# Two more groups of products summed to one chunk on VectorE, a new written order, and x tiles split over two queues

## The chip, the cores and the metric

The kernel runs on one core of a Trainium2 chip. The core has TensorE (PE: matmuls, and their weight loads, PEld), VectorE (DVE), ScalarE (ACT), GpSimd (POOL) and SyncE (SP, which issues most of the DMAs). Each works through its own queue of instructions in order and waits on semaphores where it needs another's result. The metric is the device time of one execution in microseconds, as a median over runs. A profiled execution has a span, from its first to its last instruction, which is a little shorter than its device time.

## The reference

With x of 2048 tokens x 512 columns in bf16, the result is x plus two branches of the same layer-normalised x:

```python
xn = _layernorm(x, axis=-1)
return x + _A_ref(xn, A_wqkv, A_wo) + _B_ref(xn, B_w_in, B_w_sp, B_b_sp, B_w_out)
```

Branch A is local dilated attention. q, k and v come from xn @ wqkv, in 32 heads of 16 columns. Each token attends to 8 tokens: itself and the seven at distances 2, 4, ... 14 before it. The logit is the dot product of q with each of the eight k over the 16 columns of a head; a softmax over the eight weighs the eight v; the result goes through wo.

Branch B is a gated MLP with a mixer over tokens. z = gelu(xn @ w_in) has 1376 columns. Its second half z2 is layer-normalised and multiplied from the left by the 2048 x 2048 matrix w_sp, with a bias per token (g = w_sp @ z2 + b_sp). The first half z1 is multiplied by g, and the product goes through w_out.

## The kernel before

Tokens stand in 16 tiles of 128. A tile's number is 4*tb + j: four token blocks tb of 512, each with four tiles j. The work is done by j ("block j" is the four tiles with the same j), in the order ORD = [1, 2, 3, 0] for the attention.

**The start** (L558 to L628) is written out by hand. Loads of x and of the q and k weights are issued first (L164 to L180): tile 0 as two halves of 64 partitions, on SP and ACT; tile 1 (tb=1, j=0) on ACT; tiles 2 and 3 of block 0 in one load on POOL; then on SP the q weights, block 1 of x, the k weights, blocks 2 and 3 of x, and w_z2. For each tile VectorE computes mean and variance (`ln_stats`, L201), ScalarE the square root (`ln_sqrt`), VectorE the reciprocal and the normalised tile (`ln_tile`). TensorE transposes it (`tr`), and ScalarE copies the transpose into xnT (`tr_copy`, L224); for later blocks a transposing DMA on SP does this (`tr_dma`). `qk_part` (L300) multiplies the q weights (m = 0, 1) or k weights (m = 2, 3) with some of the token blocks, in two halves cc of four chunks kc each, and `qk_copy` takes the result out of PSUM. Block 0 has the tiles 0 to 3 of the load above in its token blocks. `warm_up` matmuls keep TensorE running before the data is there.

**The rest** follows the string ORDER (L42), a list of steps, which L682 to L686 walk through. Every step issues its instructions on its engine, so ORDER is each engine's queue. A name has a letter for the step and numbers for its piece:

- On TensorE: `z` (matmuls of z2 for one tile), `X` (of z1), `q` (q or k of a block), `V` (v, eight pieces), `L` (logits), `G` (w_sp times z2 for one output tile; `G0.b` is a quarter of it), `O`, `Or`, `Oh` (the output: attention part, the rest and the main part of w_out).
- On ScalarE: `zg`, `Xg` (gelu out of PSUM), `zs` (squares for the variance), `qc`, `Vc`, `Lc` (copies out of PSUM), `Gi` (adds the bias), `E` (exp).
- On VectorE: `p` (products of q with four shifted k, for one group g and chunk c), `a`, `b` (pair adds, below), `nw`, `st` (small steps from sums to 1/std of z2), `N` (normalises a tile of z2), `M`, `S`, `R` (softmax), `U` (z1 times g), `A` (attention weights times v, 15 operations for each block), `F` (adds x to the output).
- On SP: `w` (transposing load of a tile of w_sp), `wo`, `late`, `xr` (loads), `T` (transposing DMA of a U), `s` (store).

**The logits.** There are eight groups g: four blocks, two halves of the eight shifts. A product tile pr has four chunks c of 128 columns. The sum over a head's 16 columns is made by TensorE (`logits`, L354): it multiplies each chunk by a 0/1 matrix, accumulating over the chunks that are left. `pair_add` (`a`) adds chunks 2, 3 onto 0, 1 on VectorE, leaving two; `pair_add2` (`b`) adds chunk 1 onto 0, leaving one. CHUNKS says how many chunks `L` still has to multiply, four matmuls for each:

```python
CHUNKS = (1, 1, 2, 2, 1, 1, 2, 2)
...
        n_c = CHUNKS[g]
        for c in range(n_c):
            for tb in range(TB):
                PE.matmul(pl[32 * tb:32 * tb + 32, :, :], rsel[:], pr[g % 3][:, c, :, tb, :],
```

So `b0`, `b1`, `b4`, `b5` stand in ORDER, and groups 2, 3, 6 and 7 have two chunks. Groups share three buffers (g % 3).

**What ties the queues together.** Matmul results go to a pool of three PSUM tiles (`z`, `X`, `q`, `V`, `G`, `O`) and one of two (`L`); a tile is free again when ScalarE or VectorE has read it. `G0.b` needs the `N` of block j = b; the other `G` need all of them. `N` needs `nw.13`, which needs all `zg` and `zs` of blocks 0 to 2. `U` n needs `Gi` n and `Xg` n; `T` n needs `U` n; `Or` and `Oh` of output block o need `T` 4o to 4o+3. `O` o needs `A` 15o+14. The w_sp tiles are loaded where q, k or logits data stood, after their last reader. exp and gelu use different tables of ScalarE, and changing from one to the other is a table load.

Of the kernel before, what the change touches and what calls it, by code (L numbers as in the profile page):

```python
# [70 lines left out]
def kernel(  # L71
# [145 lines left out]
    def tr(i):  # L217
        j, tb = i % 4, i // 4
        pt = ps_aux.tile([P, C, P], BF16, name="pt", tag="aux")
        for c in range(C):  # L220
            PE.transpose(pt[:, c, :], xall[:, j, tb, c * P:(c + 1) * P], ident[:])
        return pt

    def tr_copy(i, pt):  # L224
        A.copy(xnT[:, :, i * P:(i + 1) * P], pt[:])  # L225

# [72 lines left out]

    def qk_part(pq, j, m, b0, b1, ccs=(0, 1), p0=None):  # L300
        sd, c0 = m // 2, 2 * (m % 2)
        p0 = b0 if p0 is None else p0
        xv = xnT[:].rearrange("p k (b j t) -> p k b j t", b=TB, j=4)
        for cc in ccs:
            for kc in range(C):
                PE.matmul(pq[:, cc, p0 * P:(p0 + b1 - b0) * P], wqk[:, sd, kc, c0 + cc:D:C],  # L306
                          xv[:, kc, b0:b1, j, :], start=(kc == 0), stop=(kc == C - 1))
# [385 lines left out]
```

## Time and profile before

| | us |
|---|---|
| Time, median of 4 runs (204.63 to 206.45) | 204.82 |
| The profiled execution's own time | 204.79 |
| Its span | 203.1 |
| VectorE idle in the span | 18.1 |
| ScalarE busy | 102.6 |
| Table load, each of 12 | 1.28 |
| DMA, mean over the span | 128 GB/s |
| TensorE clock granted | 1.0 throughout |

In a row of the timeline, the columns are the start and the length in microseconds, the engine, the line of the kernel, the operation, out<-in with the shape, the number of instructions merged, and in brackets the idle time before it with what ended it. TensorE's matmuls are pipelined, so that the length of one is longer than its step; the distance from one start to the next is what a matmul costs in a row of them. Line numbers of the changed kernel are up to 8 higher.

### The profile page before, as it was taken

The numbers are of one execution on the slowest core, as the hardware profiler recorded it, in microseconds if no ns is written. First come the engines' busy times: TensorE is split into PE (matmuls) and PEld (weight loads), VectorE is DVE, ScalarE is ACT, GpSimd is POOL, SyncE is SP. The second block draws the span as 40 slices with busy tenths as digits, with TensorE's granted clock in tenths as the row PEclk, the third lists the DMA queues.
The fourth block names the chain that finished last, engine by engine and source line by source line (L and its number), as shares of the span: only waits on it lengthen the run. The fifth ranks groups of instructions, "written<-read, shape, count | busy, mean of one in ns | idle before, by whom it ended". The sixth has DMA issues, their size and how long they took to land.

```text
span 203.1 us, 4065 instructions
## 1 busy us (share of the span) xinstructions
PE 197.6 (97%) x1683; PEld 125.0 (62%) x1683; DVE 185.0 (91%) x263; ACT 102.6 (51%) x163; POOL 18.2 (9%) x15
## 2 busy tenths in 40 slices
PE   7899999999999999999999999999999999999993
PEld 2589856555666666666566666666654544664561
DVE  4989799999999999999899999999999999998504
ACT  3665978978999986923732273596230010021000
POOL 5000000799300000000000000000000000000000
PEclk9999999999999999999999999999999999999999
DMA  4972457900000397248990974969900384474463
GB/s 140 360 261 60 97 103 248 206 0 3 0 0 3 67 205 156 66 95 220 218 135 14 179 167 110 233 143 186 223 1 3 97 172 87 134 212 92 118 184 103
DMA packets 65826, 25.91 MB, mean 128 GB/s; under 512 B 56208, under 2 KB 65488, under 8 KB 65552
## 3 DMA queue, kind: packets, MB, share of 16 engines
q1 hardware_dynamic: 65360, 25.12, 55.3%
q0 software_dynamic: 80, 0.26, 0.5%
q8 instruction: 13, 0.21, 0.5%
q10 hardware_dynamic: 368, 0.27, 0.4%
q14 instruction: 5, 0.04, 0.1%
HBM read 10.13 MB, written 2.10 MB: 60 GB/s over the span
## 4 chain that ended last, share of the span: by engine, by line
PE 83%; DMA 6%; SPq 4%; DVE 3%; issue 2%; ACT 0%; DVEq 0%
PE pg L449 35%; PE pz L235 18%; PE pq L306 12%; PE pv L410 7%; PE po L521 4%; DMA r_w<-in_A_wqkv_dram 4%; PE po L497 4%; SPq L474 2%; PE pl L360 1%; DMA r_uz<-r_uz 1%; DVE r_pr L428 1%; DVE r_qk L511 1%; DMA out_dram<-r_qk 1%; SPq L469 1%; SPq L516 1%
## 5 line engine op out<-in xcount | busy, mean ns | idle before, releaser
L449 PE MATMUL pg<-z,r_qk 128*128 128x344 bf16 x448 | 67.0, 309 | 0.0
L449 PEld LDWEIGHTS <-r_qk 128*128 128x128 bf16 x448 | 43.8, 98 | 21.8
L235 PE MATMUL pz<-w_z,xnT 128*128 128x344 bf16 x256 | 40.0, 309 | 0.0
L424 DVE TENSOR_TENSOR r_pr<-r_x,r_w 128x2048 bf16<-128x2048 bf16 x32 | 38.3, 1221 | 1.2 <-PE pl L360 0.8
L455 ACT ACTIVATE gs<-pg,b_col 128x688 bf16<-128x688 f32 x16 | 13.3, 831 | 41.3 <-PE pg L449 31.7
L428 DVE TENSOR_TENSOR r_pr<-r_pr 128x2048 bf16<-128x2048 bf16 x28 | 33.9, 1218 | 0.0
L235 PEld LDWEIGHTS <-xnT 128*128 128x128 bf16 x256 | 24.9, 98 | 13.3 <-issue 0.8
L306 PE MATMUL pq<-xnT,r_w 128*128 128x256 bf16 (+1 forms) x176 | 28.7, 316 | 0.5 <-ACT xnT L225 0.3
L340 DVE TENSOR_TENSOR r_pr<-r_qk 128x2048 bf16<-128x2048 bf16 x24 | 28.0, 1221 | 0.0
L306 PEld LDWEIGHTS <-r_w 128*128 128x128 bf16 x184 | 20.2, 114 | 7.9 <-DMA r_w<-in_A_wqkv_dram 0.9
L297 ACT ACTIVATE r_uz<-pz 128x688 bf16<-128x688 f32 x16 | 11.7, 742 | 20.8 <-PE pz L235 20.6
L634 POOL CAST b_col<-b 128x16 f32<-128x16 bf16 x1 | 15.3, 15342 | 32.8 <-DMA b<-in_B_b_sp_dram 32.8
L316 ACT CAST r_qk<-pq 128x1024 bf16<-128x1024 f32 (+1 forms) x16 | 15.4, 990 | 4.7 <-PE pq L306 4.4
L521 PE MATMUL po<-r_w,r_uz 128*128 128x512 bf16 x70 | 15.8, 380 | 0.0
L511 DVE TENSOR_TENSOR r_qk<-po,r_qk 128x512 bf16<-128x512 f32 x14 | 9.1, 685 | 6.7 <-PE po L521 6.7
L497 PE MATMUL po<-r_lg,r_pr 32*128 32x512 bf16 x224 | 14.5, 375 | 0.0
L410 PE MATMUL pv<-xnT,r_w 128*32 128x512 bf16 x256 | 14.4, 380 | 0.0
L521 PEld LDWEIGHTS <-r_uz 128*128 128x128 bf16 x85 | 8.0, 98 | 9.8 <-issue 1.5
L349 DVE TENSOR_TENSOR r_pr<-r_pr 128x4096 bf16<-128x4096 bf16 x6 | 13.6, 2286 | 0.0
L259 ACT ACTIVATE junk<-z 128x688 bf16<-128x688 bf16 x16 | 12.5, 780 | 0.1
L253 ACT ACTIVATE z<-pz 128x688 bf16<-128x688 f32 x16 | 11.7, 739 | 1.5 <-PE pz L235 1.5
L203 DVE BATCH_NORM_STATS2 stats<-r_x 128x6 f32<-128x512 bf16 x16 | 10.7, 671 | 1.7 <-DMA r_x<-in_A_x_dram 1.7
(82 smaller groups left out, 177.0 us busy)
## 6 DMA issues: line engine op xcount, KB each, us to landing
r_qk<-in_A_x_dram SPq DMA_DIRECT2D x16, 128.0 KB, 2.4
r_lg<-in_A_wo_dram SPq DMA_DIRECT2D x8, 256.0 KB, 4.3
out_dram<-r_qk SPq DMA_DIRECT2D x15, 128.0 KB, 1.8
r_w<-in_A_wqkv_dram SPq DMA_DIRECT2D x3, 512.0 KB, 4.9
r_x<-in_A_x_dram SPq DMA_DIRECT2D x3, 512.0 KB, 6.2
w_z<-in_B_w_in_dram SPq DMA_DIRECT2D x2, 688.0 KB, 5.4
r_w<-in_B_w_out_dram SPq DMA_DIRECT2D x1, 640.0 KB, 5.4
r_x<-in_A_x_dram POOLq DMA_DIRECT2D x1, 256.0 KB, 3.9
```

The lines of the kernel that those rows point to most:

```text
L235: PE.matmul(pz[:, hh, 0:FHALF], xnT[:, kc, i * P:(i + 1) * P], wz[:, kc, hh * FHALF:(hh + 1) * FHALF], start=(kc == 0), stop=(kc == C - 1))
L306: PE.matmul(pq[:, cc, p0 * P:(p0 + b1 - b0) * P], wqk[:, sd, kc, c0 + cc:D:C], xv[:, kc, b0:b1, j, :], start=(kc == 0), stop=(kc == C - 1))
L316: cast = A.copy(dst, pq[:, :, p0 * P:(p0 + b1 - b0) * P].rearrange("p c (b t) -> p c b t", b=b1 - b0))
L340: prod = V.tensor_tensor(pr[g % 3][:, c].rearrange("p w b t -> p b w t"), q3.unsqueeze(2).broadcast_to([P, TB, 4, P]), k4, ALU.mult)
L349: V.tensor_tensor(pr[g % 3][:, 0:2], pr[g % 3][:, 0:2], pr[g % 3][:, 2:4], ALU.add)
L410: PE.matmul(pv[32 * tb:32 * tb + 32, dd, :], wv[:, kc, 2 * d2 + dd, :], xnT[:, kc, tb * TBS:(tb + 1) * TBS], start=(kc == 0), stop=(kc == ...
L424: V.tensor_tensor(pw_t[n], vp[:, :, off:off + P], a_sb[:, slot_w(w), ts].unsqueeze(1).broadcast_to([P, DH, P]), ALU.mult)
L428: V.tensor_tensor(pw_t[n] if dst is None else dst, pw_t[n], pw_t[m], ALU.add)
L449: PE.matmul(pg[:, hh, 0:FHALF], wsp[n][:, k, :], z2[:, k, hh * FHALF:(hh + 1) * FHALF], start=(k == 0), stop=(k == NT - 1))
L497: PE.matmul(pc, op[32 * tb:32 * tb + 32, d, o * P:(o + 1) * P], wo_r[32 * tb:32 * tb + 32, d, cs], start=(d == 8), stop=False, tile_positi ...
L521: PE.matmul(pc, uT[:, o % 2, m, tb * P:(tb + 1) * P], wout[:, m, cs], start=False, stop=(m == MCH - 3))
L634: G.tensor_copy(b_col[:], b16[:])
```

## The change

Three things change. CHUNKS has one chunk for groups 2 and 3 too, so the steps `b2` and `b3` come in and `L2` and `L3` have four matmuls instead of eight. ORDER is written anew. And the start is changed: tiles 0 and 1 of block 0 are loaded as halves of 256 columns, one half on SP and one on ACT; tiles 2 and 3 on ACT instead of POOL; the statistics of tiles 0 and 1 are made by halves; the transposes of tiles 0 and 1 are issued before their copies, and the copy of tile 1 is in two; the first q matmuls take chunks 0 and 1 before 2 and 3; and the matmuls for token block 2 of the first two q pieces, which were together with block 3, are put ahead of the k weights' first use.

```diff
-CHUNKS = (1, 1, 2, 2, 1, 1, 2, 2)
+CHUNKS = (1, 1, 1, 1, 1, 1, 2, 2)
 ORDER = """
-z1.3 z0.0 p1.1 z1.1 zg1.3 p0.0 zg0.0 q2.0 zg1.1 p0.1 q2.2 qc2.0 p1.0 p1.3 q2.3 qc2.2 p0.3 z3.1 p0.2 qc2.3
-zs1.1 z0.3 p1.2 zg3.1 z1.2 a0 w0 zg0.3 zs1.3 z1.0 zs0.3 a1 q3.1 zg1.2 w3 zg1.0 halo q2.1 zs0.0 b0 qc3.1 p2.0
-z2.2 qc2.1 b1 z2.0 p2.2 V0 zg2.0 p2.3 zg2.2 zs2.0 L1 L0 z0.1 Vc0 p3.3 Lc0 q3.3 p3.0 zs1.2 zg0.1 p2.1 q3.0
-qc3.3 p3.1 z0.2 a2 qc3.0 zs2.2 z2.3 zg0.2 q3.2 p3.2 zs1.0 zg2.3 a3 z3.0 qc3.2 z3.2 zg3.0 p4.3 zs2.3 z2.1 zg3.2
-p4.1 z3.3 zs0.2 p4.0 zg2.1 X3 zg3.3 nw.0 p4.2 X5 Xg3 nw.1 a4 Lc1 X4 Xg5 zs0.1 L2 zs2.1 V4 p5.3 zs3.1 st.0 Xg4
-nw.2 V3 nw.3 p5.2 Vc4 nw.4 p5.0 zs3.2 L3 V2 zs3.0 nw.5 nw.6 nw.7 Vc3 nw.8 nw.9 nw.10 p5.1 Lc2 V5 Lc3 nw.11 b4
-w4 Vc2 V1 nw.12 Vc5 a5 w2 zs3.3 V7 Vc1 nw.13 st.1 b5 w1 V6 Vc7 N0.0 N1.2 st.2 N1.0 N0.2 L4 L5 N0.3 X7 N1.1
-st.3 N2.0 st.4 Vc6 N0.1 X6 N1.3 N3.1 late N2.3 N3.2 G0.0 N3.0 Xg7 M0.0 G0.1 Xg6 N2.1 M0.1 N2.2 X1 M0.2 N3.3
-p7.1 G0.2 Xg1 M0.3 Lc4 G0.3 p7.3 G1 p6.0 E0 p7.2 Gi0 p6.3 Lc5 p6.2 G4 Gi1 w7 S0.0 p7.0 w6 p6.1 S0.1 xr0 S0.2
-G3 a7 S0.3 S0.4 Gi4 w5 a6 w10 R0 X0 Gi3 U4 L7 T4 L6 G2 A0 Xg0 Lc6 w8 U1 Lc7 U3 U0 A1 A2 X2 Gi2 mask M1.0 G5
...
-A22 Gi9 wo0.3 wo0.2 A23 Xg14 A24 U7 A25 S1.4 T7 X8 Gi14 A26 wo1.2 X9 wo0.0 wo0.1 A27 w12 G10 A28 Xg9 R1 Xg8
-A29 w13 A30 X13 A31 G11 Xg13 A32 Gi10 A33 U8 A34 A35 X11 Gi11 A36 O0 Xg11 A37 A38 U14 A39 Or0 Oh0.0 A40 A41
-Oh0.1 F0.0 U10 s0.0 F0.1 G13 F0.2 T8 A42 s0.1 F0.3 A43 s0.3 xr1 U11 A44 O1 w15 U9 A45 Gi13 A46 A47 Or1 Oh1.0
-A48 Oh1.1 F1.0 F1.1 A49 s1.1 s0.2 G12 T11 A50 A51 F1.2 F1.3 s1.2 s1.0 A52 xr2 X15 A53 G15 Xg15 A54 T10 Gi12
-A55 s1.3 T9 A56 U12 O2 Gi15 U15 U13 T15 A57 T13 A58 Or2 Oh2.0 T12 A59 Oh2.1 F2.0 F2.1 s2.1 T14 O3 F2.2 F2.3
-xr3 s2.0 Or3 s2.3 Oh3.0 s2.2 Oh3.1 F3.0 F3.1 s3.1 s3.0 end
+z1.2 z0.0 p1.3 z2.2 zg1.2 p1.0 zs1.2 q2.0 zg0.0 p0.2 zg2.2 z0.3 p0.3 zs2.2 q2.2 p1.2 qc2.0 zg0.3 p0.0 z0.2
+qc2.2 p1.1 zs0.0 z1.1 p0.1 zg0.2 z0.1 zg1.1 a1 q2.3 zg0.1 zs0.1 p2.0 q2.1 zs1.1 qc2.3 a0 halo z3.3 qc2.1 z1.3
+zg3.3 p2.2 zs0.2 z2.3 b1 zg1.3 z2.1 zg2.3 b0 z2.0 zg2.1 p2.3 zs0.3 z1.0 p2.1 zg2.0 L0 zs2.3 L1 z3.1 p3.2 zg1.0
+zs1.3 q3.2 nw.0 p3.0 zg3.1 nw.1 a2 Lc1 q3.0 qc3.2 zs2.1 z3.2 p3.3 qc3.0 zs2.0 q3.3 p3.1 zg3.2 p4.0 w1 zs1.0
+q3.1 qc3.3 nw.2 p4.1 w0 X0 nw.3 qc3.1 a3 z3.0 Xg0 w3 Lc0 X3 nw.4 b2 zg3.0 X1 nw.5 b3 w2 V6 nw.6 Xg1 nw.7 p4.3
+Xg3 zs3.3 nw.8 p4.2 L2 V2 Lc2 nw.9 Vc6 nw.10 a4 L3 zs3.0 V1 zs3.2 nw.11 st.0 Lc3 p5.2 V7 Vc2 nw.12 b4 zs3.1 V5
+Vc1 st.1 nw.13 M0.0 st.2 Vc7 p5.1 L4 V3 N2.0 M0.1 p7.3 st.3 Vc5 V0 N1.0 Vc3 M0.2 N1.2 N1.1 st.4 V4 N2.3 Vc0
+N0.3 N3.2 N1.3 N0.2 X2 N0.1 Vc4 N3.1 N0.0 X4 N3.0 N2.1 p7.2 G0.0 N2.2 p6.2 G0.1 Xg4 Xg2 N3.3 G0.2 p5.0 X5 p5.3
+G0.3 p6.0 w4 G1 M0.3 Gi0 Xg5 late p6.3 a5 E0 p6.1 G3 Gi1 w7 Lc4 U0 S0.0 w6 a6 X7 Gi3 b5 G2 p7.0 S0.1 p7.1 S0.2
+a7 S0.3 S0.4 L6 L5 G4 Lc6 U1 T0 R0 wo1.0 U3 Xg7 w9 A0 Gi2 Lc5 A1 T1 A2 L7 G7 Lc7 T3 Gi4 mask A3 w10 A4 M1.0
+wo1.2 A5 X9 Gi7 U4 A6 T4 X11 U2 G6 w8 Xg11 A7 Xg9 A8 w5 A9 A10 xr0 G9 M1.1 Gi6 A11 M1.2 A12 M1.3 A13 X6 w15
+A14 G8 Xg6 A15 Gi9 A16 A17 E1 X8 S1.0 wo0.2 Gi8 wo0.3 wo1.1 X12 A18 wo0.0 T2 G10 A19 A20 Xg12 Xg8 U9 A21 wo0.1
+S1.1 wo1.3 U7 X10 A22 Gi10 G15 U6 A23 T6 S1.2 w13 A24 A25 S1.3 w14 S1.4 G5 R1 A26 Xg10 T7 Gi15 A27 A28 A29 O0
+Gi5 w11 A30 A31 U5 Or0 A32 Oh0.0 A33 U8 Oh0.1 F0.0 F0.1 U10 G13 F0.2 F0.3 A34 xr1 A35 s0.2 A36 T5 X15 A37 Gi13
+s0.0 w12 G11 A38 Xg15 A39 T8 A40 s0.1 A41 s0.3 T9 A42 O1 Gi11 A43 U11 A44 Or1 A45 Oh1.0 A46 Oh1.1 F1.0 F1.1
+U15 G12 F1.2 T15 A47 A48 F1.3 A49 xr2 X13 A50 s1.0 G14 A51 Xg13 s1.3 s1.2 Gi12 T10 A52 U12 A53 T12 A54 T11 X14
+Gi14 A55 O2 Xg14 A56 U14 A57 T14 A58 s1.1 Or2 Oh2.0 A59 Oh2.1 F2.0 F2.1 U13 T13 O3 F2.2 F2.3 s2.3 s2.0 xr3 Or3
+Oh3.0 s2.1 s2.2 Oh3.1 F3.0 F3.1 s3.0 s3.1 end
 """
...
@@ -146,7 +146,7 @@
     warm = sb.tile([P, P], BF16, name="warm")
     b16 = sb.tile([P, NT], BF16, name="b16")
     b_col = sb.tile([P, NT], F32, name="b_col")
-    stats = sb.tile([P, NT, 6], F32, name="stats")
+    stats = sb.tile([P, NT, 12], F32, name="stats")
     mv = sb.tile([P, NT, 2], F32, name="mv")
     rstd = sb.tile([P, NT], F32, name="rstd")
     zsum = sb.tile([P, NT], F32, name="zsum")
@@ -161,17 +161,17 @@
     k_casts = [[] for _ in range(4)]
     k_reads = [[] for _ in range(4)]
 
-    def load_x0(E, tb, p0=0, p1=P):
-        E.dma_start(xall[p0:p1, 0, tb, :], x2[tb * TBS + p0:tb * TBS + p1, :])
+    def load_x0(E, tb, h):
+        E.dma_start(xall[:, 0, tb, 256 * h:256 * h + 256], x2[tb * TBS:tb * TBS + P, 256 * h:256 * h + 256])
 
     def load_wqk(E, s):
         E.dma_start(wqk[:, s],
                     A_wqkv[:, s * D:(s + 1) * D].rearrange("(k p) f -> p k f", p=P))
 
-    load_x0(SP, 0, 0, 64)
-    load_x0(A, 0, 64, P)
-    load_x0(A, 1)
-    G.dma_start(xall[:, 0, 2:4, :], xblk[0][:, 2:4, :])
+    for tb in range(2):
+        load_x0(SP, tb, 0)
+        load_x0(A, tb, 1)
+    A.dma_start(xall[:, 0, 2:4, :], xblk[0][:, 2:4, :])
     load_wqk(SP, 0)
     SP.dma_start(xall[:, 1], xblk[1])
     load_wqk(SP, 1)
@@ -198,10 +198,12 @@
                         fill=NEG, base=-DIL * slot_w(4 * h), pattern=[[DIL, 4], [1, HALO]], channel_multiplier=0)
 
 
-    def ln_stats(i):
+    def ln_stats(i, parts=1):
         j, tb = i % 4, i // 4
-        V.bn_stats(stats[:, i, :], xall[:, j, tb, :])
-        V.bn_aggr(mv[:, i, :], stats[:, i, :])
+        w = D // parts
+        for h in range(parts):
+            V.bn_stats(stats[:, i, 6 * h:6 * h + 6], xall[:, j, tb, w * h:w * h + w])
+        V.bn_aggr(mv[:, i, :], stats[:, i, 0:6 * parts])
 
     def ln_sqrt(sl):
         A.activation(rstd[:, sl], mv[:, sl, 1], ACT.Sqrt, bias=eps_t[:])
@@ -221,8 +223,8 @@
             PE.transpose(pt[:, c, :], xall[:, j, tb, c * P:(c + 1) * P], ident[:])
         return pt
 
-    def tr_copy(i, pt):
-        A.copy(xnT[:, :, i * P:(i + 1) * P], pt[:])
+    def tr_copy(i, pt, c0=0, c1=C):
+        A.copy(xnT[:, c0:c1, i * P:(i + 1) * P], pt[:, c0:c1, :])
 
     def tr_dma(i):
         j, tb = i % 4, i // 4
@@ -297,12 +299,12 @@
         A.activation(z1u[:, n % NZ1, z:z + FH].rearrange("p (a b) -> p a b", a=2),
                      tiles.pop(("x", n))[:, :, 0:FHALF], ACT.Gelu_apprx_tanh)
 
-    def qk_part(pq, j, m, b0, b1, ccs=(0, 1), p0=None):
+    def qk_part(pq, j, m, b0, b1, ccs=(0, 1), p0=None, kcs=range(C)):
         sd, c0 = m // 2, 2 * (m % 2)
         p0 = b0 if p0 is None else p0
         xv = xnT[:].rearrange("p k (b j t) -> p k b j t", b=TB, j=4)
         for cc in ccs:
-            for kc in range(C):
+            for kc in kcs:
                 PE.matmul(pq[:, cc, p0 * P:(p0 + b1 - b0) * P], wqk[:, sd, kc, c0 + cc:D:C],
                           xv[:, kc, b0:b1, j, :], start=(kc == 0), stop=(kc == C - 1))
 
@@ -556,11 +558,14 @@
     i2, i3 = blk(2), blk(3)
     warm_up(10)
     for n in range(2):
-        ln_stats(t0[n])
+        ln_stats(t0[n], 2)
         ln_sqrt(col(t0[n]))
     for n in range(2):
         ln_tile(t0[n])
-        tr_copy(t0[n], tr(t0[n]))
+    tr_copy(t0[0], tr(t0[0]))
+    pt1 = tr(t0[1])
+    tr_copy(t0[1], pt1, 0, 2)
+    tr_copy(t0[1], pt1, 2, 4)
     warm_up(1)
     warm_up(1, 2)
     for n in range(2, 4):
@@ -569,11 +574,14 @@
     for n in range(2, 4):
         ln_tile(t0[n])
     pqs = [qk_tile() for _ in range(3)]
-    qk_part(pqs[0], 0, 0, 0, 2)
+    qk_part(pqs[0], 0, 0, 0, 2, kcs=range(2))
+    qk_part(pqs[0], 0, 0, 0, 2, kcs=range(2, 4))
     tr_copy(t0[2], tr(t0[2]))
     qk_part(pqs[1], 0, 1, 0, 2, (0,))
     tr_copy(t0[3], tr(t0[3]))
     qk_part(pqs[1], 0, 1, 0, 2, (1,))
+    qk_part(pqs[0], 0, 0, 2, 3)
+    qk_part(pqs[1], 0, 1, 2, 3)
     qk_part(pqs[2], 0, 2, 0, 2)
     for n in range(2):
         ln_stats(i1[n])
@@ -584,7 +592,7 @@
     ln_apply(i1[1])
     ln_stats(i1[3])
     for n in range(2):
-        qk_part(pqs[n], 0, n, 2, 4)
+        qk_part(pqs[n], 0, n, 3, 4)
         qk_copy(pqs[n], 0, n)
     ln_sqrt(slice(9, 16, 4))
     ln_stats(i2[0])
```

More of the change, by code (lines that the diff above doesn't have):

```diff
@@ L52 @@
-G3 a7 S0.3 S0.4 Gi4 w5 a6 w10 R0 X0 Gi3 U4 L7 T4 L6 G2 A0 Xg0 Lc6 w8 U1 Lc7 U3 U0 A1 A2 X2 Gi2 mask M1.0 G5
-Xg2 A3 A4 A5 A6 X12 M1.1 Gi5 w11 A7 G6 Xg12 A8 wo1.0 w9 A9 M1.2 A10 wo1.1 A11 G7 Gi6 U5 M1.3 T5 U6 A12 E1 A13
-G8 U2 Gi7 A14 T2 A15 T6 S1.0 A16 X10 Gi8 w14 S1.1 X14 A17 T1 A18 G9 Xg10 S1.2 wo1.3 A19 T3 A20 S1.3 A21 T0 G14
-A22 Gi9 wo0.3 wo0.2 A23 Xg14 A24 U7 A25 S1.4 T7 X8 Gi14 A26 wo1.2 X9 wo0.0 wo0.1 A27 w12 G10 A28 Xg9 R1 Xg8
-A29 w13 A30 X13 A31 G11 Xg13 A32 Gi10 A33 U8 A34 A35 X11 Gi11 A36 O0 Xg11 A37 A38 U14 A39 Or0 Oh0.0 A40 A41
```

## The prediction

> **What bounds the kernel now.** I read the page's busy shares first, then the chain that ended last, then TensorE's and VectorE's timelines where the change acts. The page:
>
> ```profile
> span 203.1 us, 4065 instructions
> PE 197.6 (97%) x1683; PEld 125.0 (62%) x1683; DVE 185.0 (91%) x263; ACT 102.6 (51%) x163; POOL 18.2 (9%) x15
> PE 83%; DMA 6%; SPq 4%; DVE 3%; issue 2%; ACT 0%; DVEq 0%
> ```
>
> TensorE is busy nearly always, with VectorE close behind, and the chain is TensorE's. A busy share can hide gaps, so I looked at stretches (columns: time, length, busy time and instructions of PE, weight loads, DVE, ACT, POOL, clock, DMA share, GB/s):
>
> ```profile
> 4.00:6.00 2.00, 1.70 (x8) 0.50 (x6) 1.86 (x8) 0.59 (x2) 0.03 (x1) 1.00 0.89 288
> 6.00:8.00 2.00, 1.53 (x16) 1.08 (x14) 1.89 (x7) 1.38 (x4) 0.00 (x0) 1.00 1.08 367
> 8.00:10.00 2.00, 1.93 (x20) 1.38 (x18) 1.93 (x6) 1.27 (x3) 0.00 (x0) 1.00 1.10 354
> 22.80:77.10 54.30, 54.30 (x522) 33.77 (x520) 52.97 (x68) 48.62 (x95) 15.58 (x2) 1.00 0.41 87
> 77.10:182.70 105.60, 105.60 (x806) 66.16 (x807) 104.04 (x125) 39.93 (x47) 0.00 (x0) 1.00 0.65 135
> ```
>
> From 22.8 to 182.7 TensorE never stops. Its steps (start to start in its timeline) are constant: a `z`, `X` or `G0.b` 1.167 us, `q` and `V` 1.727, one chunk of an `L` 0.217, `G` 4.667, `O` 3.456, `Oh` 2.165. Adding them in the old order gives every start to within 0.1 us, if a change to the narrow matmuls of `L`, `V`, `O` and back costs 0.1 us each way. So the end is TensorE's first useful work, plus its steps, plus the tail. Only two things move the time: TensorE's work, and any wait that the new order makes for it.
>
> At the start it does wait:
>
> ```profile
> 7.40 1.03 PE L306 MATMUL pq<-xnT,r_w 128*128 128x256 bf16 x8 [0.35 <-ACT xnT L225]
> 9.33 0.60 PE L306 MATMUL pq<-xnT,r_w 128*128 128x256 bf16 x4
> 10.11 3.25 PE L306 MATMUL pq<-xnT,r_w 128*128 128x256 bf16 x28 [0.18 <-DMA r_w<-in_A_wqkv_dram]
> ```
>
> The first matmuls wait for x's transpose copy; those at 10.11 wait for the K weights, having been free from 9.77. From 10.11 there is no gap.
>
> **Summing to one chunk in groups 2 and 3.** TensorE drops one chunk from `L2` and `L3`: 2 x 4 = 8 matmuls at 0.054, 0.43 us less (one chunk is 0.217). VectorE gains `b2` and `b3`:
>
> ```profile
> 67.93 1.22 DVE L352 TENSOR_TENSOR r_pr<-r_pr 128x2048 bf16<-128x2048 bf16 x1
> 69.07 0.16 DVE L271 SCALAR_TENSOR_TENSOR zm<-zm,zvar 128x12 f32<-128x12 f32 x1
> ```
>
> The step is 1.137, so 2.27 us more on VectorE. That is free only while TensorE isn't waiting for it.
>
> **The new order.** TensorE's amount of work is unchanged, but narrow matmuls now come in four runs before `O0` (L0 L1; V6 to V4; L6 L5; L7) where there were three: +0.2 us.
>
> Does TensorE wait? I add each queue's steps along the new order and compare them where they meet.
>
> *The first spatial matmuls.* `G0.0` needs the four `N0`. TensorE reaches it at 22.79 + 21 x 1.167 (z, X) + 16 x 1.727 (q, V) + 5 x 0.217 + 0.4 (two narrow runs) = 76.4. (The same sum for the old order gives 77.1; the chain has it at 77.13.) VectorE begins its products at 24.96, then 23 products at 1.137, 5 pair adds at 2.2, 5 single adds, 12 `N` at 0.37, three `M0` 1.14 and 17 small ones 1.7: 75.1. It waits some 0.45 more: `nw.0` for the last gelu and `nw.2` for the square `zs1.0`, 0.15 each by ACT's own sum, and `p3.2` for `L0`, 0.1. So 75.5; margin 0.9. That `b2` and `b3` stand ahead of `N` is paid by `a5`, `b5`, `p5.0` and `p5.3` going behind it. Before, the last `N0` ended at 75.75, a margin of 1.4. `G0.2` and `G0.3` have 0.8 and more.
>
> *The middle.* VectorE's exponent sum `S1.0` waits about 0.4 us for `E1`, which stands on ACT behind `Xg6`, `Gi9` and a table load of 1.28. VectorE is not yet needed there. ACT loads tables 10 times instead of 12, none in TensorE's way: the PSUM tile taken three allocations earlier is always read 0.3 us or more before its reuse. SP's queue has stretches where an item holds others (`w15` waits for `G9`, then four loads of `wo` for `E1`, then `T2`), but `T2` is needed some 7 us after it lands, and the spatial weights arrive 3 us or more early (landing 4.3 to 6.3 us after issue).
>
> *The end.* VectorE's `A59` would start at 185.4 unhindered, 186.9 with 1.5 us of waits (the above, and the output adds F0 and F1 waiting for TensorE), and ends at 188.1; `O3` needs it at 190.8. Before it was:
>
> ```profile
> 184.67 3.61 DVE L428 TENSOR_TENSOR r_pr<-r_pr 128x2048 bf16<-128x2048 bf16 x3
> 189.02 1.29 DVE L511 TENSOR_TENSOR r_qk<-po,r_qk 128x512 bf16<-128x512 f32 x2 [0.73 <-PE po L521]
> 191.07 0.39 PE L497 MATMUL po<-r_lg,r_pr 32*128 32x512 bf16 x2
> ```
>
> done at 188.28 for 191.07. The narrowest place is new: `U13` now stands behind F2.0 and F2.1, which wait for `Oh2.0`. From that end: 0.16 drain, 0.6 + 0.6 for the adds, 0.6 for `U13`, 2.65 for transpose `T13` (landings 2.6 to 2.8) make 4.6, while TensorE has `Oh2.1` and `O3`, 5.6, before `Or3`. Margin 1.0.
>
> So the order costs 0.2 and makes no wait, by margins of 0.9 and 1.0 us.
>
> **The start.** The halves add two statistics instructions; one of 512 columns takes 0.66[...], so two halves cost about 0.1 more per tile (0 to 0.2), and VectorE's chain is 0.2 later. The copy of tile 1 in halves gives its first two chunks 0.25 earlier, so the first q matmuls stay near 7.35. The transposes of tiles 2 and 3 move from 8.44 to about 8.6 and from 9.11 to 9.3, and the 0.88 us of matmuls on tile 2 now come before the K weights are needed: TensorE reaches the K part at 10.8, where the old order would stand at 10.11 + 0.88 = 10.99. Gain 0.17; from a loss of 0.3 (x later) to a gain of 0.5 (all idle time closed).
>
> The weights: SP issues one load more ahead of both, 0.60 us by the row of the old half tile, while x tiles 2 and 3 leave POOL's queue for ACT's. The Trainium skill (DMA: Bandwidth & Descriptors, Issuing engines are not separate DMA queues) says that issuing from several engines saves only the sequencer's time. By it the Q weights land 0.6 later, 7.67 for 7.07. By the rows the engines moved 288 GB/s from 4 to 6 and 367 later, so there was room and they land less late. Either way q matmuls from 7.67 would end at 8.5, before tile 2's transpose: nothing. K weights, 10.07, have until 10.8.
>
> Thirty-two matmuls of 128 columns replace sixteen of 256 (0.108 each, 1.74). No 128-column matmul with these strided weights is in the trace. The nearest row is the transposes, 128 wide with a weight load each, 0.056 apart; the strided load reads 113 ns for 98. That bounds it from 0.056 to 0.071; I take 0.060, +0.19. A rule speaks against the change: the Trainium skill (TensorE: Matmul & The Clock Gate, Back-to-back issue gap) has a stream of weight load and 128-column matmul sustained at about 81 ns. By it 2.6 us instead of 1.74, +0.85. The trace differs (0.056), so it is a rival.
>
> **Sum.** 204.79 (profiled execution, span 203.1) - 0.43 + 0.20 - 0.17 + 0.19 = 204.58; the median is 204.82, 0.03 off: 204.6. A 1% difference (2.05 us) is about what a measurement of this kernel can tell, so this is no change.
>
> **Rivals.**
> *The start gains more* (0.15): x arrives earlier on two hardware queues, and TensorE's idle 0.35 and 0.34 both close. 0.6 less: 204.0. For it: GB/s is low up to 6 us. Against: VectorE's chain, not x, paces tiles 2 and 3.
> *Narrow matmuls at the rule's pace* (0.10): 205.3.
> *VectorE becomes the bound* (0.23), slower: VectorE reaches `N0.0` late and `G0.0` waits. It decides from 0.9 us beyond my sum, and each microsecond more is lost in full, since TensorE has no idle time afterwards. Were VectorE's waits ahead of it the 3.1 us that the whole old run has (187.06 traced for `A59`, 183.96 summed) instead of 0.45, it would be 1.7 us late: 206.3; with a second loss at `U13` of like size, 207.5 or more. For it: 2.27 us more on an engine at 91%, and margins cut. Against: ACT's sums show short waits.
> *The forecast* (0.52): 204.2 to 205.0.
>
> Faster by over 1% would need 2 us off TensorE, of which the start holds 0.7 and `L` 0.43: 0.03. Slower by over 1%: the worse two thirds of the VectorE rival, 0.15. Range 203.8 to 206.6.
>
> **What would show it.** Right: L362 with 40 matmuls; no idle time of PE between 22.8 and the output's tail; `G0.0` near 76.4; the K part not waiting for its DMA; last `po` matmul 0.2 earlier. Wrong: idle of PE at L451 after DVE L291, or at L508 after a transpose; matmuls at L308 of 128 columns more than 0.07 apart; the first q matmuls later than 7.7.

## The result, and the profile after

| | before | after |
|---|---|---|
| Median, us | 204.83 (204.22 to 207.13, 57 runs) | 203.98 (203.49 to 205.56, 36 runs) |
| Ratio to before, 95% interval | | 0.9958 [0.9947, 0.997] |
| The profiled execution's own time, us | 204.79 | 204.69 |
| Its span, us | 203.1 | 203.0 |

The changed kernel is 0.4% faster: 0.86 us by the ratio (0.61 to 1.09). The forecast was 204.6. The profiled execution of after is not a typical one. It took 0.7 us more than the median, and what it lost is in its first ten microseconds. A second profile of the same kernel (e4_repeat, below) took 204.02 and shows the usual start. So I read the rest of the kernel from the first profile, and the start from both.

The page of after, its head and its chain:

```profile
span 203.0 us, 4074 instructions
PE 197.4 (97%) x1691; PEld 124.9 (62%) x1691; DVE 187.1 (92%) x267; ACT 100.1 (49%) x162; POOL 11.2 (6%) x14
PE 94%; DMA 3%; DVE 1%; ACTq 0%; DVEq 0%; issue 0%
```

TensorE has 8 matmuls more: 16 from splitting token block 2 off, less 8 of `L`. VectorE is busy 2.1 us longer, about what `b2` and `b3` take. POOL has one instruction less and 7 us less of work. The chain is TensorE's again, now for 94% of the span.

The stretches of after, with the columns of the table shown before:

```profile
4.00:6.00 2.00, 2.00 (x10) 0.79 (x9) 1.69 (x7) 0.59 (x3) 0.00 (x0) 1.00 1.02 346
6.00:8.00 2.00, 1.36 (x12) 0.98 (x11) 1.12 (x3) 1.33 (x4) 0.00 (x0) 1.00 1.08 373
8.00:10.00 2.00, 1.31 (x16) 1.03 (x15) 1.89 (x7) 0.84 (x3) 0.00 (x0) 1.00 1.10 351
22.80:77.10 54.30, 54.30 (x515) 33.92 (x514) 53.27 (x75) 49.94 (x96) 9.39 (x2) 1.00 0.36 77
77.10:182.70 105.60, 105.60 (x804) 65.86 (x801) 103.84 (x121) 36.46 (x44) 0.00 (x0) 1.00 0.67 141
```

The two long stretches read as they did before: TensorE busy for the whole of both, and VectorE close behind. What costs is 6 to 10 us, where TensorE works 1.36 and 1.31 us instead of 1.53 and 1.93. Its timeline says on what it waits there:

```profile
7.35 1.06 PE L308 MATMUL pq<-xnT,r_w 128*128 128x256 bf16 x8 [0.64 <-DMA r_w<-in_A_wqkv_dram]
9.11 0.40 PE L223 MATMUL pt<-ident,r_x 128*128 128x128 bf16 x4 [0.69 <-DVE r_x L216]
9.34 0.60 PE L308 MATMUL pq<-xnT,r_w 128*128 128x256 bf16 x4
9.78 0.39 PE L223 MATMUL pt<-ident,r_x 128*128 128x128 bf16 x4
10.00 3.70 PE L308 MATMUL pq<-xnT,r_w 128*128 128x256 bf16 x48
```

The row at 10.00 has no bracket, so the wait for the K weights is gone, as forecast. In its place there are a wait of 0.64 for the Q weights and one of 0.69 for VectorE's normalised tile 2. VectorE's timeline leads that back to a load:

```profile
2.95 0.75 DVE L205 BATCH_NORM_STATS2 stats<-r_x 128x6 f32<-128x256 bf16 x2 [1.13 <-DMA r_x<-in_A_x_dram]
5.39 0.41 DVE L216 TENSOR_SCALAR r_x<-r_x,mv,rstd 128x512 bf16<-128x512 bf16 x1
6.85 0.69 DVE L205 BATCH_NORM_STATS2 stats<-r_x 128x6 f32<-128x512 bf16 x1 [1.04 <-DMA r_x<-in_A_x_dram]
```

Tiles 0 and 1 came earlier than in before (first statistics at 2.95 for 3.55), tiles 2 and 3 later: VectorE had been free for 1.04 us when they landed at 6.82.

Two readings split each run in two: when the first `z` matmul starts (22.79 in before), and how far from there the last matmul of the kernel starts. The first is the start's doing, the second that of ORDER and CHUNKS. A ratio compares with executions of before taken beside that kernel (their medians: 204.70 to 204.83) and is not the quotient of the medians, which for e1 is 1.0003 and for e9 0.9970.

| kernel | first z | z to last matmul | `G0.0` | first q | tiles 2, 3 landed | Q weights landed | profiled time | median | ratio [95%] |
|---|---|---|---|---|---|---|---|---|---|
| before | 22.79 | 176.56 | 77.13 | 7.40 | 5.17 | 7.07 | 204.79 | 204.83 | |
| after | 23.13 | 176.36 | 76.82 | 7.35 | 6.82 | 7.30 | 204.69 | 203.98 | 0.9958 [0.9947, 0.997] |
| e1_order_only | 22.44 | 176.35 | 76.13 | 7.60 | 5.18 | 6.69 | 204.53 | 204.81 | 0.9988 [0.9962, 1.0014] |
| e2_start_only | 22.86 | 176.90 | 77.20 | 7.17 | 6.56 | 7.12 | 204.95 | 204.9 | 0.9999 [0.9979, 1.0019] |
| e3_x23_pool | 22.09 | 176.36 | 75.78 | 6.81 | 5.18 | 6.69 | 204.12 | 204.22 | 0.9966 [0.9949, 0.9983] |
| e4_repeat | 22.13 | 176.36 | 75.82 | 6.85 | 5.22 | 6.71 | 204.02 | 204.02 | 0.9966 [0.9951, 0.9981] |
| e5_act_first | 24.06 | 176.35 | 77.75 | 8.18 | 4.78 | 7.40 | 206.45 | 205.93 | 1.0053 [1.0037, 1.0069] |
| e6_sp_first | 27.47 | 176.36 | 81.16 | 9.03 | 9.41 | 6.58 | 209.05 | 207.69 | 1.0144 [1.0116, 1.0172] |
| e7_before_t14 | 22.78 | 176.56 | 77.11 | 7.81 | 5.37 | 6.92 | 204.81 | 204.56 | 0.9991 [0.998, 1.0002] |
| e8_dve_plus | 22.77 | 177.74 | 77.86 | 6.96 | 6.47 | 6.67 | 205.94 | 205.61 | 1.0028 [1.0012, 1.0045] |
| e9_x23_sp | 22.25 | 176.35 | 75.94 | 7.04 | 4.82 | 6.33 | 204.14 | 204.11 | 0.9956 [0.9939, 0.9973] |
| e10_no_b23 | 21.88 | 177.22 | 76.00 | 6.73 | 4.73 | 6.27 | 204.23 | 204.64 | 0.9992 [0.9981, 1.0003] |
| e11_x23_sp_old_order | 22.06 | 176.89 | 76.40 | 6.92 | 4.96 | 6.44 | 204.16 | 204.43 | 0.998 [0.9967, 0.9992] |
| e12_no_23 | 22.48 | 176.36 | 76.17 | 6.95 | 4.51 | 6.43 | 204.49 | 204.84 | 0.9992 [0.9978, 1.0007] |

From the last matmul's start to the end of the span it is another 3.4 to 4.3 us, so a single profile places a time no closer than some tenths. Nor do the medians and ratios: for one kernel the two differ by up to 0.3 us.

### The profile page after: what moved, and what is told of

Read it like the earlier page. It is cut to its first block, busy times and chain, and to the rows that moved or that the text cites. A ratio compares the mean times of both kernels' runs of the same rounds, so it can differ in the third digit from the quotient of the medians.

```text
span 203.0 us, 4074 instructions
## 1 busy us (share of the span) xinstructions
PE 197.4 (97%) x1691; PEld 124.9 (62%) x1691; DVE 187.1 (92%) x267; ACT 100.1 (49%) x162; POOL 11.2 (6%) x14
## 4 chain that ended last, share of the span: by engine, by line
PE 94%; DMA 3%; DVE 1%; ACTq 0%; DVEq 0%; issue 0%
PE pg L451 37%; PE pz L237 18%; PE pq L308 13%; PE po L523 8%; PE pv L412 7%; PE po L499 6%; DMA r_x<-in_A_x_dram 3%; PE pl L362 1%; PE pa L523 1%; PE po L508 1%; PE pb L499 1%; DVE stats L205 1%; PE pt L223 1%; PE pa L308 0%; ACTq L165 0%; PE pb L523 0%
## 5 line engine op out<-in xcount | busy, mean ns | idle before, releaser
L308 PE MATMUL pq<-xnT,r_w 128*128 128x256 bf16 (+2 forms) x192 | 28.8, 304 | 0.6 <-DMA r_w<-in_A_wqkv_dram 0.6
L342 DVE TENSOR_TENSOR r_pr<-r_qk 128x2048 bf16<-128x2048 bf16 x24 | 28.5, 1220 | 0.0
L205 DVE BATCH_NORM_STATS2 stats<-r_x 128x6 f32<-128x512 bf16 (+1 forms) x18 | 10.9, 612 | 2.2 <-DMA r_x<-in_A_x_dram 2.2
L412 PEld LDWEIGHTS <-r_w 128*32 128x32 bf16 x256 | 9.4, 138 | 4.6 <-issue 0.3
```

Source lines behind the costliest of these rows:

```text
L342: prod = V.tensor_tensor(pr[g % 3][:, c].rearrange("p w b t -> p b w t"), q3.unsqueeze(2).broadcast_to([P, TB, 4, P]), k4, ALU.mult)
L412: PE.matmul(pv[32 * tb:32 * tb + 32, dd, :], wv[:, kc, 2 * d2 + dd, :], xnT[:, kc, tb * TBS:(tb + 1) * TBS], start=(kc == 0), stop=(kc == ...
```

## The experiments

**The two halves of the change, one at a time.** e1 is before with the new CHUNKS and ORDER; e2 is after with the old ones. Their edits:

```diff
 e1_order_only, against before
-CHUNKS = (1, 1, 2, 2, 1, 1, 2, 2)
+CHUNKS = (1, 1, 1, 1, 1, 1, 2, 2)
-z1.3 z0.0 p1.1 z1.1 zg1.3 p0.0 zg0.0 q2.0 zg1.1 p0.1 q2.2 qc2.0 p1.0 p1.3 q2.3 qc2.2 p0.3 z3.1 p0.2 qc2.3
+z1.2 z0.0 p1.3 z2.2 zg1.2 p1.0 zs1.2 q2.0 zg0.0 p0.2 zg2.2 z0.3 p0.3 zs2.2 q2.2 p1.2 qc2.0 zg0.3 p0.0 z0.2
...
 e2_start_only, against after
-CHUNKS = (1, 1, 1, 1, 1, 1, 2, 2)
+CHUNKS = (1, 1, 2, 2, 1, 1, 2, 2)
...
```

> The new CHUNKS and the new order alone, with the start of before. Theory A (TensorE does 0.43 us less, 0.2 more for one more change to narrow matmuls, no wait): 0.2 us faster than before, about 204.6. Rival (the whole measured gain of 0.85 us comes from the order): 204.0. Rival (the order makes VectorE late and the start hides it): slower than before.

> The new start alone, with the CHUNKS and the order of before. Theory A (the rest of the gain is the start's, and the profiled execution with tiles 2 and 3 landing at 6.8 us is an unlucky one): 0.6 us faster than before, about 204.2. Rival (the order gives all): as before, 204.8, or 0.3 slower as in the profile of after, 205.1.

e1's stretch from first z to last matmul is 176.35 for before's 176.56. That 0.2 us is the order's worth, and it returns to 0.01 us in every run that has both the new CHUNKS and the new order and no added work. The medians cannot show so little: 0.9988 holds 1. e2 shows two things at once. Its start was no better than before's (22.86), with tiles 2 and 3 landing late, as in after's first profile. And its old order took 176.90, 0.34 more than in before. The waits of e2 from 183 us to the end name the place:

```profile
PEld L508 <- DMA r_uz<-r_uz: 0.4, 1, 0.4
```

That is `Or3` waiting for the last transpose, here `T14`. It comes back below.

**Where do tiles 2 and 3 lose their time?** e3 puts their load on POOL's queue again; e4 is after, unchanged, for a second profile.

```diff
 e3_x23_pool, against after
-    A.dma_start(xall[:, 0, 2:4, :], xblk[0][:, 2:4, :])
+    G.dma_start(xall[:, 0, 2:4, :], xblk[0][:, 2:4, :])
```

> After, with x tiles 2 and 3 loaded from POOL's queue again. If ACT's queue sharing the engines with the q weights is what makes VectorE wait 1.04 us for tile 2 in the profile of after, tile 2 lands near 5.2 us as before, VectorE goes on at about 5.8 and the time is up to 0.6 us below after. If POOL's slow packets hold the q weights up (they began only after 4 us in before), the first q matmuls move to 7.5 or later and the time is as after or up to 0.5 above.

> After unchanged, beside the other three on one chip. 203.98 us as measured, and a second profile: if the late landing of tiles 2 and 3 (6.82 us) is one execution's chance, it lands up to 1 us earlier here and TensorE's z matmuls start at 22.2 to 22.8; if it is the rule, again near 6.8 and 23.1.

The repeat started differently from the first profile, with nothing changed. TensorE's timeline of e4_repeat:

```profile
6.85 1.03 PE L308 MATMUL pq<-xnT,r_w 128*128 128x256 bf16 x8
8.11 0.40 PE L223 MATMUL pt<-ident,r_x 128*128 128x128 bf16 x4 [0.22 <-DVE r_x L216]
8.34 0.60 PE L308 MATMUL pq<-xnT,r_w 128*128 128x256 bf16 x4
8.78 0.39 PE L223 MATMUL pt<-ident,r_x 128*128 128x128 bf16 x4
9.00 3.70 PE L308 MATMUL pq<-xnT,r_w 128*128 128x256 bf16 x48
```

Everything from tile 2's transpose on is 1.00 us earlier than in after's first profile, and its tiles 2 and 3 landed at 5.22. The only difference I found ahead of that is which of two loads was issued first. SyncE's timelines and ScalarE's (both give the queue's issues), first of after, then of e4_repeat:

```profile
1.73 0.43 SPq L168 DMA_DIRECT2D r_w<-in_A_wqkv_dram  x1
1.74 0.46 ACTq L174 DMA_DIRECT2D r_x<-in_A_x_dram  x1
```

```profile
1.71 0.46 ACTq L174 DMA_DIRECT2D r_x<-in_A_x_dram  x1
1.74 0.44 SPq L168 DMA_DIRECT2D r_w<-in_A_wqkv_dram  x1
```

In after the Q weights (SP) were issued 6 ns ahead of tiles 2 and 3 (ACT), in e4 34 ns behind them. e2 and e8 have SP first too, by 13 and 6 ns, and their tiles landed at 6.56 and 6.47. The packets show the effect on either load. With SP first, the packets of the Q weights begin at 2.92 to 3.05 and those of tiles 2 and 3 at 3.85 to 4.00; in e4 it is the other way round, 4.17 and 2.93. So in four profiles of this start, the load that was issued second was the one held back, by about 1 us. The cost is unequal: with ACT first the Q weights lose nothing that matters (6.71, still ahead of before's 7.07), with SP first tiles 2 and 3 lose 1.2 to 1.6 us.

e3 has no such pair of loads: on POOL's queue the tiles land at 5.18 and z begins at 22.09, the same as e4's good start. Moving this load from POOL to ACT therefore gains nothing over e3's start, and costs when SP comes first.

**Forcing the order.** e5 was to put ACT's load first always, e6 SP's, by one more issue on the other queue: tile 1's half in two pieces of 64 partitions.

```diff
 e5_act_first, against after (e6_sp_first splits ACT's half of tile 1 instead)
-    for tb in range(2):
-        load_x0(SP, tb, 0)
-        load_x0(A, tb, 1)
+    load_x0(SP, 0, 0)
+    load_x0(A, 0, 1)
+    load_x1_64(SP, 0)
+    load_x0(A, 1, 1)
```

> After, with SP's half of tile 1 loaded as two issues of 64 partitions, so that SP issues the q weights some 0.4 us later and ACT's load of tiles 2 and 3 (issued at 1.74 us within 0.03 us of the q weights in every profile so far) is surely first. Theory C (whichever of the two is issued first keeps the other's data back by 0.7 us, and it is a toss in after): tiles 2 and 3 land near 5.2 us in every execution, z matmuls start at 22.1 to 22.2, 203.9 us and no executions near 204.7. Rival (the late tiles come from something else, such as other traffic): the same two groups of times as after. Rival (the later q weights cost what they are late): q matmuls 0.4 later, 204.3.

> After, with ACT's half of tile 1 loaded as two issues of 64 partitions, so that ACT issues tiles 2 and 3 some 0.4 us later and SP's q weights are surely first. Theory C: tiles 2 and 3 land at 6.6 to 7.0 us always, VectorE waits over 0.8 us for them, z matmuls start at 22.9 to 23.2, 204.7 us. Rival: as after, 204.0.

Both missed, by 2 and 3 us, because the added piece became a victim itself. In e5 tile 1's second piece stood on SP behind ACT's load of tiles 2 and 3, and landed at 4.96, after them (4.78). In e6 it stood on ACT behind SP's Q weights and landed at 6.35, tiles 2 and 3 only at 9.41. The direction of the rule held; as a measure of the two starts these runs say nothing, since tile 1 was moved as well. A second loss came on top. TensorE stood idle for 1.09 us ahead of its first transposes in e5 and for 2.27 in e6 (0.42 in e4), and the q matmuls behind them ran at half the pace. Eight of them, in e5 and then in e6:

```profile
8.18 1.89 PE L314 MATMUL pq<-xnT,r_w 128*128 128x256 bf16 x8
9.03 1.86 PE L314 MATMUL pq<-xnT,r_w 128*128 128x256 bf16 x8
```

In e4 the same eight took 1.03, 0.109 apart; here they are 0.213 apart. The granted clock of e6 was 0.5 from 8.53 to 15.36 us and 1.0 from there to the tail, which is why its z to last matmul is 176.36 like the others'. e5's clock is on record only from 10.23 us, where it is 1.0 and the matmuls are 0.109 apart again. In the other twelve profiles that idle time is at most 0.65 and the eight are 0.109 apart. Whether the idle time brought the clock down no run tries, but 2 and 3 us are not what the order of two loads costs.

**One queue instead of a toss.** e9 puts tiles 2 and 3 on SP, ahead of the Q weights.

```diff
 e9_x23_sp, against after
-    A.dma_start(xall[:, 0, 2:4, :], xblk[0][:, 2:4, :])
+    SP.dma_start(xall[:, 0, 2:4, :], xblk[0][:, 2:4, :])
     load_wqk(SP, 0)
```

> After, with the load of tiles 2 and 3 on SP's queue, between SP's half of tile 1 and the q weights; ACT has only its two halves. One queue now holds the two loads whose order was a toss (issued 6 to 34 ns apart). Theory C: tiles 2 and 3 always land near 5.2 us and the q weights near 6.7 to 7.0, z matmuls start at 22.1 to 22.2, 203.9 us, and the group of executions near 204.7 is gone. Rival (the q weights, 0.46 us later in SP's queue, then hold TensorE): 0.3 to 0.5 slower than after.

The tiles landed at 4.82, VectorE did not wait for them, and the executions lay closer together: 203.74 to 204.38 in 13 runs, where after has 203.49 to 205.56 in 36. With so few runs that is a hint; e10 and e11, with the same loads, spread over 0.8 and 0.9 us in 22 runs each, e4 over 1.4 in 22. But the median, 204.11, is not below after's. Most executions of after seem to have drawn the good start already: 30 of its 36 are at or below 204.5, and e4's profile, with that start, took 204.02. How often each start is drawn I cannot tell: three of the four profiles with this pair of loads have the bad one.

**What the matmuls of token block 2 ahead of the K weights are worth.** e12 is e9 with those matmuls back behind them.

```diff
 e12_no_23, against e9_x23_sp
-    qk_part(pqs[0], 0, 0, 2, 3)
-    qk_part(pqs[1], 0, 1, 2, 3)
...
-        qk_part(pqs[n], 0, n, 3, 4)
+        qk_part(pqs[n], 0, n, 2, 4)
```

> As the run with tiles 2 and 3 on SP, with the matmuls of token block 2 back behind the first use of the k weights (together with block 3, as in before). If they fill a wait for the k weights, TensorE waits 0.2 to 0.5 us for them again and z starts that much later. If the gain of the start is the earlier tiles 0 and 1 alone, no difference (0.05 at 16 weight loads less).

TensorE's timeline of e12_no_23, and then of e9_x23_sp:

```profile
9.80 3.25 PE L308 MATMUL pq<-xnT,r_w 128*128 128x256 bf16 x28 [0.23 <-DMA r_w<-in_A_wqkv_dram]
```

```profile
9.06 3.76 PE L308 MATMUL pq<-xnT,r_w 128*128 128x256 bf16 x48
```

Without them the wait for the K weights is back, in the profile with 0.23, and z begins 0.23 later (22.48 for 22.25). The medians lie 0.73 apart, but e12's executions spread from 203.98 to 205.68; I hold 0.23 shown and leave the rest open.

**The order under the start without a toss.** e10 is e9 with groups 2 and 3 in two chunks, the rest of the new order kept. e11 is e9's start with the whole old order.

```diff
 e10_no_b23, against e9_x23_sp
-CHUNKS = (1, 1, 1, 1, 1, 1, 2, 2)
+CHUNKS = (1, 1, 2, 2, 1, 1, 2, 2)
-q3.1 qc3.3 nw.2 p4.1 w0 X0 nw.3 qc3.1 a3 z3.0 Xg0 w3 Lc0 X3 nw.4 b2 zg3.0 X1 nw.5 b3 w2 V6 nw.6 Xg1 nw.7 p4.3
+q3.1 qc3.3 nw.2 p4.1 w0 X0 nw.3 qc3.1 a3 z3.0 Xg0 w3 Lc0 X3 nw.4 zg3.0 X1 nw.5 w2 V6 nw.6 Xg1 nw.7 p4.3
```

> As the run with tiles 2 and 3 on SP, with b2 and b3 taken out and two chunks for groups 2 and 3 as in before; the rest of the new order stays. Theory A (eight matmuls at 0.054, and VectorE's additions are covered): z start to last matmul 176.78 instead of 176.35, 0.43 us slower than that run. Rival (VectorE's additions cost somewhere): the same or faster.

> As the run with tiles 2 and 3 on SP, with the CHUNKS and the order of before: the new start without its toss, alone. Theory C (the start is worth 0.6 to 0.7 us when tiles 2 and 3 land early, whatever the order, and the start alone showed nothing because they landed late): z matmuls start at 22.1 to 22.2, 204.2 us. Rival (the gain of the start needs the new order): 204.7 to 204.9 again.

e10's median is 0.53 above e9's. Its profile has 177.22 from z to the last matmul, 0.87 more than e9: the eight matmuls (0.43, as forecast) and a wait at `Or3`. Without the wait it would be 176.78, 0.22 above before's 176.56, and that is the price of the new order's fourth run of narrow matmuls, forecast at 0.20. The end of its chain (start, length, what):

```profile
190.14 4.12 DMA r_uz<-r_uz
194.92 2.28 PE po L523 x10
```

`T13` took 4.12 us to be released here. e9 issued its `T13` at 190.08, needed it at about the same time, and did not wait. e11 has the same wait at `Or3` as e2 (176.89): its start is 0.73 earlier than before's and its end 0.33 later, 0.40 by the profile and 0.41 by its ratio. Between e11 and e9 lies the order: 0.32 by the medians, where 0.2 is TensorE's work. Their profiles differ by 0.54, so not every execution of e11 need have the wait.

**The last transpose earlier.** e7 is before with `T14` moved ahead of `A59`, so that `Or3` has it long before.

```diff
 e7_before_t14, against before
-... T12 A59 Oh2.1 F2.0 F2.1 s2.1 T14 O3 F2.2 F2.3
+... T12 T14 A59 Oh2.1 F2.0 F2.1 s2.1 O3 F2.2 F2.3
```

> Before, with the transpose T14 issued ahead of the wait for F2.1 and of the store s2.1 instead of behind them. In the profile of the start alone TensorE waits 0.33 us for T14 at Or3; in the profile of before it doesn't. If most executions of before have that wait, this is up to 0.3 us faster than before (204.5); if not, the same (204.8).

0.9991 [0.998, 1.0002] doesn't tell it from before. In the profile of before this wait wasn't there, nor is it in e7's, so e7 could only gain in executions in which it comes.

**VectorE's margin.** e8 adds two VectorE operations ahead of `N2.0` that compute something not used, 1.22 us each.

```diff
 e8_dve_plus, against after
-Vc1 st.1 nw.13 M0.0 st.2 Vc7 p5.1 L4 V3 N2.0 M0.1 ...
+Vc1 st.1 nw.13 M0.0 st.2 Vc7 p5.1 L4 V3 d d N2.0 M0.1 ...
+    def dummy_add():
+        half = [r_w[:, n * 1024:(n + 1) * 1024].rearrange("p (a b) -> p a b", a=4) for n in range(2)]
+        V.tensor_tensor(smt[:], half[0], half[1], ALU.add)
```

> After, with two idle additions of 1.2 us each on VectorE just ahead of the first N (their result is overwritten later). The profile of after has a margin of 1.13 us between the end of N0.0 and the start of G0.0. Theory A (that margin is the point from which VectorE decides, and what lies beyond it is lost in full): TensorE waits about 1.2 us at G0.0, z start to last matmul is 177.55 instead of 176.35, about 1.2 us slower than after. Rival (a wait at G0.0 is made up later, since VectorE isn't needed on time): 0 to 0.3. Rival (more than the margin, as VectorE's lateness reaches the end too): 2.4.

TensorE's timeline about `G0.0`, of after and then of e8_dve_plus:

```profile
75.80 1.18 PE L237 MATMUL pz<-w_z,xnT 128*128 128x344 bf16 x7
76.82 1.48 PE L451 MATMUL pg<-z,r_qk 128*128 128x344 bf16 x9
```

```profile
75.74 0.89 PE L237 MATMUL pz<-w_z,xnT 128*128 128x344 bf16 x5
77.86 1.91 PE L451 MATMUL pg<-z,r_qk 128*128 128x344 bf16 x12 [1.23 <-DVE z L291]
```

The two additions take 2.39 us of VectorE (69.14 to 71.53 in its timeline), and the last matmul came 1.38 later. So 1.0 us was absorbed. The rest was lost in full: `G0.0` came 1.40 later after the first z, and the last matmul 1.38 later, so nothing was made up behind it. e8's ratio is 0.0070 above after's, 1.4 us. The margin read from after's profile fits: its last `N0` ended at 75.69, 1.13 before `G0.0`, and in e8 0.15 pass from that end (77.71) to `G0.0` (77.86), which leaves 0.98.

## Why the prediction was right, and where it was not

The measured 203.98 lies in the stated range of 203.8 to 206.6, near its lower end and below the 204.2 to 205.0 that got the largest chance. The parts on TensorE and VectorE came as forecast; the part on the start was too small by half a microsecond. The prediction also took 1% for the least that a measurement can tell here. The interval of 0.9947 to 0.997 tells a difference of 0.4%.

**The order and the sum in groups 2 and 3: as forecast.** The sum had -0.43 for eight matmuls and +0.20 for one more run of narrow ones, -0.23. The profiles give -0.20. L362, the `L` matmuls, has 40, and there is no idle time from the first z to the last matmul.

**VectorE as the bound: refuted, with the margin forecast.** The rival needed VectorE 0.9 us late at `G0.0`. Nothing of it appeared in any run of the new order without added work. The forecast margin was 0.9; the profiles of the changed CHUNKS and order have 1.13 to 1.15, and e8 used it up at 1.0. The small waits counted beforehand were there and short, `nw.0` 0.08, `nw.2` 0.07, `S1.0` 0.54; one of 0.51 at `mask` was not counted. Beyond the margin the loss is whole, as e8 shows.

**The margin at `Or3`: right in size, but not safe.** The forecast gave `U13`, `T13` and then `Or3` 1.0 us, with `T13` landing after 2.65. After fits that: `T13` was issued at 190.96 and `Or3` began at 194.67, 1.06 beyond a landing after 2.65. But e10 waited there in the new order, since its `T13` took 4.12. "Landings 2.6 to 2.8" left out what before's trace had: of the eight transposes whose landing it tells, three took 3.47, 3.70 and 4.24. The last section has the cause.

**Narrow matmuls: nearer to the row than I took them.** In after's trace the 128-column matmuls with strided weights stand 0.056 apart: 32 x 0.056 = 1.79 for the old 16 x 0.109 = 1.74, so +0.05 where I had +0.19. The rule of the Trainium skill (TensorE: Matmul & The Clock Gate, Back-to-back issue gap), 81 ns for a sustained stream of weight load and matmul, would have made it 2.6. That rival is refuted; the trace's nearest row, the transposes at 0.056, was the right one.

**The start: the term that was mis-sized.** The sum had -0.17 for the start and +0.19 for the narrow matmuls, nothing together. In e4, whose time is the median, the first z starts 0.66 earlier than in the profile of before (22.13 for 22.79). TensorE's rows divide that in two. The matmuls just ahead of the K weights' first use start 0.33 earlier (9.00 for 9.33). And the wait behind them, from 9.77 to 10.11 in before, is gone: 0.34. The second half was forecast, less some 0.17 for a later chain. The step that failed is "VectorE's chain is 0.2 later", and with it "the transposes of tiles 2 and 3 move from 8.44 to about 8.6": the transposes of tile 2 moved to 8.11. VectorE's rows, two of before and two of e4, have the first statistics and the normalising of tile 1:

```profile
3.55 0.69 DVE L203 BATCH_NORM_STATS2 stats<-r_x 128x6 f32<-128x512 bf16 x1 [1.73 <-DMA r_x<-in_A_x_dram]
5.86 0.41 DVE L214 TENSOR_SCALAR r_x<-r_x,mv,rstd 128x512 bf16<-128x512 bf16 x1
```

```profile
3.09 0.75 DVE L205 BATCH_NORM_STATS2 stats<-r_x 128x6 f32<-128x256 bf16 x2 [1.28 <-DMA r_x<-in_A_x_dram]
5.53 0.41 DVE L216 TENSOR_SCALAR r_x<-r_x,mv,rstd 128x512 bf16<-128x512 bf16 x1
```

The prediction took the arrival of tiles 0 and 1 as unchanged and charged VectorE for the extra statistics. But the tiles came earlier: the first statistics began at 2.81 to 3.14 in the eleven profiles with column halves, for 3.44 to 3.55 in the three with the old loads, and VectorE waits for a DMA in all of them. Two halves of 256 columns are issued in 0.87 to 0.90 us on each queue, where one half of 64 partitions took SP 0.60 in before, and ACT, whose second issue was a whole tile, needed 1.19 for its two. The Q weights were therefore issued 0.27 later (1.74 for 1.47), not 0.60, and landed earlier, at 6.71 for 7.07. The extra instructions cost less than I gave them (a half alone takes 0.37 in e6, a whole tile 0.66): 0.46 of an earlier arrival left 0.33 at the end of tile 1, so 0.13 for the two tiles, for 0.2. e3 has the same start as e4 (first z at 22.09) with POOL's load kept, so the gain is not that of the move off POOL. No run has the column halves alone.

With the copy in two, the first q matmul starts at 6.85, 0.55 earlier. That gained nothing by itself: TensorE then waits 0.22 for tile 2, since VectorE sets the pace there.

So the rival that I gave 0.15, "the start gains more", 204.0, is what came: x earlier, and both of TensorE's idle times closed, though only the second counted. The objection that I put against it, that VectorE's chain and not x paces tiles 2 and 3, held in e4 but not in after's first profile, where x paces them after all. 0.66 and the order's 0.20 make 0.86, and the medians differ by 0.85. That they agree so closely is luck, since the old start spreads too: e1, with the start of before, did not wait for the K weights and has its first z at 22.44.

**What was not thought of** is that the start would differ from one execution to the next. The margin on which it turns, 6 to 34 ns between two issues, is not in the profile of before, where SP and ACT issue at other times and tiles 2 and 3 have POOL's queue.

## What to carry to other kernels

Before you price a split load, read how long each queue's issues take and when the first reader could start: loads split along columns instead of partitions came with first statistics half a microsecond earlier, of which 0.33 reached TensorE, more than all the planned order gained. Then look for the engine that sets the pace: a first matmul 0.55 earlier gained nothing while TensorE waited for VectorE behind it. Two large loads on two queues that are issued at the same instant were a toss here; the load that is needed first belongs ahead of the other in the same queue, if steadiness counts. A margin counted on an engine's queue is worth trying out by added work: e8 found 1.0 where the sum had given 0.9, while the margin that rested on a DMA's landing did not hold in every run.
